# Batch 3's tail tokens by crossbar transpose, in a kernel whose engine orders are written out

## The chip, the cores and the metric

The kernel runs on one core of a Trainium2 chip. The metric is the device time of one execution in microseconds (us). The core has a matrix engine (PE, with its weight loads shown as PEld), a vector engine (DVE), an activation engine (ACT), a general engine (POOL) and a sync engine (SP); SP, ACT and POOL issue DMAs.

## The reference

A sliding-window attention with linear biases feeds an RWKV channel mix. B=8 batches, H=8 heads, S=576 tokens, head size 64; the model width is 512, the inner width 1024.

```python
scores = scale * np.matmul(q, k.transpose(0, 1, 3, 2))
mask = (rel >= 0) & (rel < window)                    # window = 128
scores = np.where(mask, scores + bias[None], -1000000000.0)
attn = np.exp(scores - max); attn = attn / (sum + 1e-09)
x = (attn @ v), heads side by side                    # [B, S, 512]
...
xk = mu_k * x + (1.0 - mu_k) * x_prev                 # x_prev: x one token earlier
xr = mu_r * x + (1.0 - mu_r) * x_prev
k = np.maximum(xk @ w_k, 0.0)
v = k * k @ w_v
r = 1.0 / (1.0 + np.exp(-(xr @ w_r)))
return (r * v)
```

## The kernel before

**Tiles.** 576 tokens are four blocks of 128 and a tail of 64. The attention works by batch and by pair of heads (`g` = 0 to 3). q and k are loaded with the tokens on the partitions, and must be transposed before the scores: batch 0 in two parts and batches 1 to 3 by transposes on PE (`qk_quad`, `qk_some`) and copies by ACT or DVE; batches 4 to 7 by crossbar transposes, which are DMAs on SP's queue (`flip`, L554). `scores` (L742 the products, L748 the biases of batch 0) gives ACT's exponentials (L766); for batches 1 to 7 DVE multiplies with a mask (L779) that ACT makes once (L1198). `attend` multiplies with v and normalizes; the result is transposed (`out_t`, `out_some`, or by crossbar, L928, for batches 5 to 7), shifted and mixed (`shift`), and `channel_mix` does the three matrix products, in 16 calls over pairs of batches. Most matmuls of the program are recorded under L395 and most transposes under L398, which are helpers, and most copies under L715.

**The tail tokens.** The 64 tail tokens of q and k of a batch are loaded by POOL's queue into `ts_buf` (L540; L534 for batch 0). Three ways turn them into `tt_buf`, which `scores` reads for the last block. Batch 0 (`TW`): 32 small matmuls on PE and two copies (`tails`). Batches in `XTT`: one crossbar transpose on SP's queue (`tail_flip`, L647), queued when the batch's loads are planned, ahead of what SP's queue gets for later batches. All others (`tails_full`): four 128x128 transposes on PE and one DVE copy (L715 `tt<-duo`). Both `ts_buf` and `tt_buf` have two buffers.

**What sets the order.** Every step is a node of a planner (`Plan`) with an engine, a planned duration, dependencies and buffers. The nodes of PE, ACT and DVE are numbered in the order in which they are made, and `ORDER` holds three lists of these numbers: each engine does its nodes in exactly that order, and where a node may run on ACT or DVE (squares, some copies), the list that holds it decides. The planner plays the lists through with its durations; from the times that come out follow the buffer numbers and the order of SP's instructions (loads and crossbar transposes in a chain, outputs as they become ready). POOL's loads are in a fixed chain. PE is planned with 0.095 us more where an operation's row grouping (64 or 128 rows of the array) differs from the one before. 82 warm-up matmuls on PE are nodes like others.

The number of hardware DMAs, `n_hw`, counts the crossbar transposes too, `len(XTT)` among them; `n_split = -n_hw % 8` row tiles, counted from the fourth last, are written out in two halves.

Of the kernel before, what the change touches and what calls it, by code (L numbers as in the profile page):

```python
# [20 lines left out]

ORDER = {
    "PE": [int(x) for x in """
# [17 lines left out]
""".split()],  # L41
    "ACT": [int(x) for x in """
# [11 lines left out]
""".split()],  # L54
    "DVE": [int(x) for x in """
# [16 lines left out]
""".split()],  # L72
}

# [168 lines left out]
def kernel(  # L243
# [14 lines left out]
    B, H, S, D = q.shape  # L258
# [15 lines left out]
    PE, ACT, DVE, POOL, SPE, FAB, VIR = "PE", "ACT", "DVE", "POOL", "SP", "FAB", "VIR"  # L274
# [39 lines left out]
    FT = (2, 3)  # L314
    KQ = ACT
    VCUT = True
    XTT = range(4, B)
    VDEP = 0
    TCOST = 1.5
    KLAST = 1  # L320
# [95 lines left out]
    def op(e, dur, deps, prio, emit, need=(), free=()):  # L416
        return plan.add(e, dur, LAT.get(e, 0.2) if isinstance(e, str) else LAT[e[0]] if len(e) == 1 else 0.22,
                        deps, prio, emit, need, free)
# [71 lines left out]
    n_ident = dve_op(0.11, emit_ident, [n_iota], (0, -1))  # L490
# [118 lines left out]
    th, tl, n_w, src1 = {}, {}, {}, {}  # L609
# [341 lines left out]
    def tails(b, prio):  # L951
        htt = Hold("tt")
        hs = th[b]
        if b in XTT:
            plan.follow(last["tt"], ttg[b])
            last["tt"] = ttg[b]
            return tth[b], ttl[b]
        if b not in TW:
            return tails_full(b, prio, htt, hs)
        hp = [Hold("p"), Hold("p")]  # L960

        def bank(r):
            return one(hp[r])[:, 0:256].rearrange("p (g i c n) -> p g i c n", g=G, i=2, n=4)

        def emit(e):
            for i in range(2):
                for n in range(4):
                    for hl, r in ((0, 0), (1, 1), (1, 0), (0, 1)):
                        rows = slice(64 * r, 64 * r + 64)
                        matmul(  # L970
                            hp[r], bank(r)[64 * hl:64 * hl + 64, :, i, :, n],
                            lhsT=ts_buf[hs.idx][rows, 4 * i + n],
                            rhs=ident[rows, rows].rearrange("p (c g t) -> p t g c", g=G, t=2)[:, hl],
                            start=True, stop=True)

        t = op(PE, 0.009 * 32, list(tl[b]) + [n_ident], prio + (0,), emit, hp, [hs])
        t.rows = (65, 65)
        g = virtual("tt", [htt])
        c = [op(DVE, dve_t(256), [t, g], prio + (0,), lambda e, r=r: copy_of(
            hp[r], e, tt_buf[htt.idx][:, :, 0:2, 32 * r:32 * r + 32],  # L980
            one(hp[r])[:, 0:256].rearrange("p (g i w) -> p g i w", g=G, i=2)),
                (), [hp[r]]) for r in range(2)]
        return htt, c
# [146 lines left out]
    for part in range(2):  # L1130
# [3 lines left out]
        for g in range(G):  # L1134
            prio = (0, 0, part, g)
# [12 lines left out]
            hp = Hold("p") if part == 0 else None  # L1148
# [15 lines left out]
            else:  # L1164
                cold = 1.8 if part == 0 and g < 2 else 1.0
                t = op(PE, (0.115 if f32 else 0.0565) * 4 * cold, cs + [n_ident], prio + (3,), emit_t,
                       [hp] + ([hq0[g]] if part == 0 else []))
# [72 lines left out]
    for b in range(1, B):  # L1240
# [4 lines left out]
        for g in range(G):  # L1245
            prio = (0, b, 0, g)
# [77 lines left out]
```

## Time and profile before

| | |
|---|---|
| median of 3 runs | 227.4 us (226.96 to 227.56) |
| the profiled execution's own time | 226.97 us |
| its span, first to last instruction | 225.1 us |
| granted PE clock | 1.00 |
| busy: PE, DVE, ACT, POOL | 217.7, 186.8, 153.0, 91.9 us |
| matmul instructions on PE | 2525 |
| tail crossbar transposes (L647), PE tail transposes of 128x128 (L398 on `ts`) | 4, 12 |

The profile's times are of one execution, counted from the start of its span. A row of the timeline gives start, length, engine, line, operation and tiles of merged instructions; matmuls are pipelined, so the length of a group runs to the modelled end of its last one, and the distance from its start to the next group's start is what it costs PE. Some matmul records are missing, which looks like a short idle time on PE.

### The profile page before, as it was taken

How to read it: one execution, taken by the hardware profiler on the slowest of the kernel's cores; microseconds unless marked ns; L12 is line 12 of the kernel's file. 1: busy time of each engine (PE TensorE's matmuls, PEld its weight loads, DVE VectorE, ACT ScalarE, POOL GpSimd, SP SyncE). 2: the span in 40 equal slices, each digit the busy share in tenths (PEclk: the TensorE clock that was granted, in tenths of full speed). 3: DMA queues.
4: the chain of work that ended last, by engine and by line, in shares of the span. 5: the costliest groups of instructions: out<-in, count | busy, mean ns of one | idle time of the engine just before them, and what ended most of it. 6: DMA issues, size and time to landing. Idle time of an engine off the chain costs nothing.

```text
span 225.1 us, 6344 instructions
## 1 busy us (share of the span) xinstructions
PE 217.7 (97%) x2525; PEld 131.5 (58%) x2555; DVE 186.8 (83%) x422; ACT 153.0 (68%) x276; POOL 91.9 (41%) x118
## 2 busy tenths in 40 slices
PE   8999999999999999999999999999999999999994
PEld 8666756756765555555665565446664655456542
DVE  5779898899768998999789996599969989957433
ACT  2488999898999886980899665843469654135801
POOL 8865726589980983374428663400000000000000
PEclk9999999999999999999999999999999999999999
DMA  7999999999999999999999999999952121243015
GB/s 169 177 186 200 195 197 175 227 146 178 185 154 148 161 149 156 150 182 133 207 207 142 152 181 155 148 180 191 206 167 76 51 57 30 79 155 126 3 41 192
DMA packets 132093, 33.85 MB, mean 150 GB/s; under 512 B 119256, under 2 KB 127712, under 8 KB 132064
## 3 DMA queue, kind: packets, MB, share of 16 engines
q0 software_dynamic: 95728, 16.26, 96.5%
q1 hardware_dynamic: 34592, 16.59, 36.6%
q10 hardware_dynamic: 1744, 0.59, 1.1%
q8 instruction: 20, 0.33, 0.6%
q14 instruction: 9, 0.07, 0.1%
HBM read 33.56 MB, written 9.44 MB: 191 GB/s over the span
## 4 chain that ended last, share of the span: by engine, by line
PE 91%; ACT 4%; DVE 2%; issue 1%; DVEq 0%
PE duo L395 77%; PE duo L742 7%; PE duo L398 4%; PE duo L748 2%; ACT at L766 1%; ACT xt L715 1%; ACT rl L1022 1%; ACT qk L715 1%; DVE ot L1054 1%; DVE qk L715 1%; ACT kk L994 0%; DVE at L779 0%; ACT rs L1040 0%; DVE tv L499 0%; DVE tt L715 0%
## 5 line engine op out<-in xcount | busy, mean ns | idle before, releaser
L1022 ACT ACTIVATE rl<-duo 128x256 bf16<-128x256 f32 (+2 forms) x104 | 47.3, 485 | 34.8 <-PE duo L395 25.1
L395 PE MATMUL duo<-xk,wk_sb 128*128 128x256 bf16 (+2 forms) x410 | 70.2, 312 | 0.3
L766 ACT ACTIVATE at<-duo 128x1024 bf16<-128x1024 f32 (+2 forms) x68 | 63.8, 987 | 8.9 <-PE duo L742 8.5
L395 PE MATMUL duo<-wv_sb,kk 128*128 128x512 bf16 (+2 forms) x281 | 66.1, 373 | 1.1 <-issue 0.5
L395 PEld LDWEIGHTS <-wk_sb 128*128 128x128 bf16 x416 | 38.9, 98 | 22.9 <-issue 0.8
L395 PEld LDWEIGHTS <-kk 128*128 128x128 bf16 x296 | 27.1, 98 | 29.8 <-issue 1.3
L779 DVE TENSOR_TENSOR at<-at,mask 128x1024 bf16<-128x1024 bf16 x56 | 37.2, 680 | 5.8 <-ACT at L766 5.7
L519 POOL DMA_DIRECT2D vs<-in_v_dram x32 | 28.4, 901 | 22.7 <-PE duo L395 16.8
L996 DVE TENSOR_TENSOR kk<-rl 128x256 bf16<-128x256 bf16 (+2 forms) x95 | 29.9, 336 | 8.4 <-ACT rl L1022 8.3
L395 PE MATMUL duo<-wr_sb,xr 128*128 128x512 bf16 x135 | 35.5, 379 | 0.5
L1040 ACT ACTIVATE rs<-duo 128x512 bf16<-128x512 f32 x36 | 21.6, 612 | 19.8 <-PE duo L395 17.1
L1054 DVE SCALAR_TENSOR_TENSOR ot<-rs,duo 128x512 f32<-128x512 bf16 (+2 forms) x37 | 24.3, 665 | 9.1 <-PE duo L395 8.9
L819 DVE TENSOR_TENSOR xu<-duo,rc 128x640 bf16<-128x640 f32 (+2 forms) x36 | 26.2, 738 | 0.4
L913 DVE SCALAR_TENSOR_TENSOR xk<-dl,mu_sb,xt 128x576 bf16<-128x576 bf16 (+1 forms) x32 | 24.6, 779 | 0.2
L913 DVE SCALAR_TENSOR_TENSOR xr<-dl,mu_sb,xt 128x576 bf16<-128x576 bf16 (+1 forms) x32 | 24.6, 778 | 0.0
L395 PEld LDWEIGHTS <-at 128*128 128x128 bf16 x576 | 21.5, 97 | 4.8 <-issue 0.3
L395 PE MATMUL duo<-vs,at 128*128 128x65 bf16 x512 | 21.7, 193 | 0.0
L395 PEld LDWEIGHTS <-xr 128*128 128x128 bf16 x144 | 13.3, 98 | 12.9 <-issue 0.4
L550 POOL DMA_DIRECT2D cb<-in_k_dram x20 | 17.8, 926 | 7.3 <-DMA vs<-in_v_dram 7.2
L550 POOL DMA_DIRECT2D cb<-in_q_dram x20 | 17.7, 931 | 5.6 <-DMA vs<-in_v_dram 2.5
L715 ACT COPY qk<-duo 128x512 bf16<-128x512 bf16 (+1 forms) x25 | 14.5, 593 | 0.4 <-PE duo L398 0.4
L906 DVE TENSOR_TENSOR dl<-xt 128x576 bf16<-128x576 bf16 (+1 forms) x32 | 13.4, 438 | 1.1 <-ACT xt L715 0.6
(73 smaller groups left out, 189.4 us busy)
## 6 DMA issues: line engine op xcount, KB each, us to landing
out_dram<-ot SPq DMA_DIRECT2D x34, 256.0 KB, 4.7
vs<-in_v_dram POOLq DMA_DIRECT2D x32, 128.0 KB, 8.5
cb<-in_q_dram POOLq DMA_DIRECT2D x20, 128.0 KB, 9.8
cb<-in_k_dram POOLq DMA_DIRECT2D x20, 128.0 KB, 11.2
wk_sb<-in_moe_w_k_dram POOLq DMA_DIRECT2D x2, 512.0 KB, 8.7
cb<-in_q_dram POOLq DMA_DIRECT2D x4, 256.0 KB, 9.7
cb<-in_k_dram POOLq DMA_DIRECT2D x4, 256.0 KB, 9.7
wv_sb<-in_moe_w_v_dram POOLq DMA_DIRECT2D x2, 512.0 KB, 12.2
```

What stands on the lines that cost most here:

```text
L395: return use(h, nc.tensor.matmul(*a, **k))
L519: return dma(POOL, 256, issue_t(1024), lambda e: nc.gpsimd.dma_start(out=vs_buf[h.idx][:, j, :, 0:D], in_=v[b, :, 128 * j:128 * j + 128].r ...
L550: return [dma(POOL, 256, issue_t(1024), lambda e, r=r: nc.gpsimd.dma_start(out=cb_buf[h.idx][:, i, r], in_=src[:, :, r]), [g], kind="q") f ...
L715: return (nc.scalar.copy if e == ACT else nc.vector.tensor_copy)(out=out, in_=in_)
L766: lambda e, ah=ah, w=w, hp=hp: nc.scalar.activation(out=ah(), in_=two(hp)[:, :, 0:w], func=AF.Exp, scale=float(scale)), (), [hp])
L779: nc.vector.tensor_tensor(out=a, in0=a, in1=m, op=ALU.mult)
L819: use(hp, nc.vector.tensor_tensor(out=out_, in0=a5()[:, :, :, 0:D], in1=rc[:, :, 0:nt, None].to_broadcast([128, 2, nt, D]), op=ALU.mult), hx)
L913: lambda e: nc.vector.scalar_tensor_tensor(out=buf[hk.idx][:, g, e0 + c0:e0 + c1], in0=dls(), scalar=mu[:, g:g + 1], in1=xc(1), op0=ALU.mu ...
L996: nc.vector.tensor_tensor(out=out, in0=in_, in1=in_, op=ALU.mult)
L1022: a = op(ACT, act_t(n), [s], pr, lambda e, hp=hp, hr=hr: use(hp, nc.scalar.activation(out=rl_buf[hr.idx][:, 0:n], in_=one(hp)[:, 0:n], fun ...
L1040: lambda e, hp=hp, hs=hs: use(hp, nc.scalar.activation(out=rs_buf[hs.idx], in_=one(hp), func=AF.Tanh, scale=0.5), hs), [hs], [hp])
L1054: use(hv, nc.vector.scalar_tensor_tensor(out=ot_buf[ho.idx][:, a:b], in0=rs_buf[hs.idx][:, a:b], scalar=1.0, in1=one(hv)[:, a:b], op0=ALU. ...
```

## The change

`XTT` takes in batch 3, so `tails(3)` returns the crossbar's result and `tails_full` is left for batches 1 and 2. The planned duration of batch 0's tail matmuls rises from 0.288 to 0.5 us; their instructions stay. With batch 3's two tail nodes gone, all numbers from 579 on fall by two, and all three lists are new: PE's has 450 numbers in place of 451, ACT's 282 in place of 281, DVE's 420 in place of 422. Nine nodes that may run on either engine go from DVE to ACT and eight the other way. The order of the late PE nodes within a batch, and of batches among each other, differs nearly everywhere by a few places; the last four nodes of PE are the same. `n_split` becomes 0.

```diff
 ORDER = {
     "PE": [int(x) for x in """
-84 109 92 74 83 70 64 40 43 115 97 106 59 80 62 102 110 47 81 100 50 65 105 91 117 103 60 77 93 49 79 112 72 63
-71 82 75 48 42 67 58 85 68 76 52 46 123 86 56 57 39 69 53 55 116 108 90 163 125 78 89 120 126 139 161 119 113
...
-221 243 279 223 192 273 264 276 209 340 226 261 258 270 328 361 343 373 295 326 313 287 331 282 376 334 364 284
...
+101 57 106 51 86 85 92 49 79 82 113 100 74 65 50 102 80 108 64 68 41 76 66 39 40 91 72 98 99 55 70 105 93 114 52
+75 58 54 59 94 107 63 118 77 61 87 47 46 104 78 123 62 67 81 97 120 112 89 110 125 126 88 115 96 56 137 161 149
...
+226 276 243 279 209 189 270 340 328 264 261 192 267 326 361 373 343 273 307 287 292 282 364 346 331 289 284 367
...
     "ACT": [int(x) for x in """
...
     "DVE": [int(x) for x in """
...
@@ -314,7 +314,7 @@
     FT = (2, 3)
     KQ = ACT
     VCUT = True
-    XTT = range(4, B)
+    XTT = range(3, B)
     VDEP = 0
     TCOST = 1.5
     KLAST = 1
@@ -973,7 +973,7 @@
                             rhs=ident[rows, rows].rearrange("p (c g t) -> p t g c", g=G, t=2)[:, hl],
                             start=True, stop=True)
 
-        t = op(PE, 0.009 * 32, list(tl[b]) + [n_ident], prio + (0,), emit, hp, [hs])
+        t = op(PE, 0.5, list(tl[b]) + [n_ident], prio + (0,), emit, hp, [hs])
         t.rows = (65, 65)
         g = virtual("tt", [htt])
         c = [op(DVE, dve_t(256), [t, g], prio + (0,), lambda e, r=r: copy_of(
```

Node 340 is the first q/k transpose group of batch 1, 343 its first scores, 123 the first transposes of batch 0, 39 to 120 the warm-ups.

82 rows, old and new, of the table ORDER are left out of this document.

## The prediction

> **What bounds the kernel now.** I read the page's busy shares and slices first, then the chain, then a table of stages, then the timeline at the places that the change touches.
>
> ```profile
> span 225.1 us, 6344 instructions
> PE 217.7 (97%) x2525; PEld 131.5 (58%) x2555; DVE 186.8 (83%) x422; ACT 153.0 (68%) x276; POOL 91.9 (41%) x118
> PE   8999999999999999999999999999999999999994
> PE 91%; ACT 4%; DVE 2%; issue 1%; DVEq 0%
> ```
>
> The matrix engine (PE) is busy in every slice and carries 91% of the chain. Work that leaves PE is worth its own time; work that leaves another engine is worth something only where PE waits for that engine. The stage table says where that can be (columns after the length: busy us and instructions of PE, weight load, DVE, ACT, POOL):
>
> ```profile
> core 0: us, PE busy (x) PEld busy (x) DVE busy (x) ACT busy (x) POOL busy (x), PEclk, DMA share, GB/s
> 0.00:13.00 13.00, 11.74 (x168) 9.68 (x168) 8.55 (x41) 5.03 (x7) 10.60 (x20) 1.00 1.30 178
> 13.00:20.00 7.00, 6.68 (x147) 4.10 (x136) 5.97 (x22) 6.13 (x16) 4.28 (x6) 1.00 1.64 189
> 20.00:25.00 5.00, 5.00 (x107) 4.39 (x109) 4.55 (x15) 4.89 (x14) 3.24 (x4) 1.00 1.56 191
> 25.00:30.00 5.00, 4.52 (x157) 3.58 (x148) 4.76 (x15) 5.00 (x14) 3.19 (x4) 1.00 1.30 205
> 30.00:45.00 15.00, 14.73 (x193) 9.38 (x194) 13.61 (x29) 13.86 (x27) 7.78 (x10) 1.00 1.71 199
> 45.00:60.00 15.00, 14.67 (x275) 8.88 (x277) 13.45 (x25) 14.26 (x29) 14.05 (x17) 1.00 2.25 166
> 60.00:90.00 30.00, 29.63 (x390) 18.00 (x394) 26.21 (x54) 25.70 (x45) 19.44 (x24) 1.00 1.89 156
> 90.00:150.00 60.00, 59.48 (x597) 33.34 (x605) 53.12 (x108) 44.69 (x70) 29.33 (x35) 1.00 1.81 167
> 150.00:221.00 71.00, 70.42 (x530) 39.65 (x538) 55.80 (x117) 33.05 (x63) 0.00 (x0) 1.00 0.48 104
> ```
>
> From 13 to 60 us PE, ACT and DVE are all about full: ACT has 5.00 of 5 us at 25 to 30 and 14.26 of 15 at 45 to 60. PE's idle time, length less busy, is 0.32 + 0.00 + 0.48 at 13 to 30, 0.27 + 0.33 at 30 to 60, and 0.37 + 0.52 + 0.58 after 60; in the first 13 us it is 1.26, most of it ahead of the first matmul. So all that new lists can win behind 13 us is about 2.9 us, and less, because a good part of the 1.47 us after 60 is records of matmuls that are missing. That ceiling matters more than anything else here: a reordered program does the same PE work.
>
> **The change part by part.** *The tail tokens of batch 3.* Four 128x128 transposes on PE and one DVE copy go, one crossbar transpose on SP's queue comes. PE and then DVE at that place:
>
> ```profile
> 59.82 0.82 PE L395 MATMUL duo<-xk,wk_sb 128*128 128x256 bf16 x6
> 60.48 0.39 PE L398 MATMUL duo<-ident,ts 128*128 128x128 bf16 x4
> 60.70 0.60 PE L395 MATMUL duo<-xk,wk_sb 128*128 128x256 bf16 x4
> 60.90 0.42 DVE L715 COPY tt<-duo 128x512 bf16<-128x512 bf16 x1
> ```
>
> The four hold PE from 60.48 to 60.70: 0.22 us, all on the path, since PE stands back to back there. The copy takes 0.42 us of DVE, in a stage in which DVE has 26.21 of 30 us: its cover is those 3.8 us of slack, and I cost its removal at nothing (at most 0.42 if DVE were the bound there). The loads of the tail tokens stay with POOL's queue.
>
> *The crossbar transpose that comes.* The landing times, a load, and the place of the consumer:
>
> ```profile
> tt<-ts SPq DMA_TRANSPOSE x4, 6.8
> qx<-cb SPq DMA_TRANSPOSE x32, 7.7
> 53.56 0.76 POOL L540 DMA_DIRECT2D ts<-in_k_dram  x1
> ts<-in_k_dram POOLq DMA_DIRECT2D x8, 64.0 KB, 8.7
> 74.93 0.47 PE L398 MATMUL duo<-ident,xu 64*128 64x64 bf16 x20
> ```
>
> Batch 3's second tail load is issued at 53.6 and by the median has landed at 62.3; 6.8 us more is 69.1. In the new PE list the first batch 3 scores that read the tail (node 596 in the new numbers) stand two places ahead of the transposes of batch 2's outputs (node 493), which the old run made at 74.93. That leaves some 5 us, so the transfer is hidden. What it stands in front of is batch 4's own crossbar queue, which is the first rival.
>
> *One output less.* `n_split` is worked out from the number of hardware DMAs; 95 becomes 96, so it goes from 1 to 0 and the fourth row tile from the end leaves in one DMA and not two. Nothing waits for either: 0.
>
> *Changes of PE's row grouping.* Going through both PE lists with the node's row counts, operations on 64 rows follow ones on 128, or the other way round, 89 times before and 92 times after. The price of one:
>
> ```profile
> 215.81 4.05 PE L395 MATMUL duo<-wv_sb,kk 128*128 128x512 bf16 x18
> 93.22 1.02 PE L395 MATMUL duo<-xk,wk_sb 128*128 128x512 bf16 x4
> 94.17 0.56 PE L742 MATMUL duo<-qx 64*128 64x256 bf16 x8
> ```
>
> Eighteen equal matmuls in 4.05 us with a last one of about 0.37 give 0.216 us from start to start. Four would be 0.865; the 64-row operation starts 0.95 after the first, so a change costs 0.09 us. Three more are +0.28. This eats what the four transposes give.
>
> [...]
>
> *The tail transposes of batch 0.* Only the planner's duration changes (0.288 to 0.5); the instructions are the same. What the shorter value cost:
>
> ```profile
> 16.01 0.65 PE L395 MATMUL duo<-ident,ts 64*64 64x32 bf16 x32
> 16.72 0.34 PE L742 MATMUL duo<-qk 64*128 64x128 bf16 x4
> 17.25 0.60 PE L748 MATMUL duo<-dist,sid 128*128 128x256 bf16 x4 [0.20 <-DVE tt L715]
> ```
>
> They hold PE for 0.47 us (16.01 to the next operation at 16.48), and the copies behind them arrive late: 0.20 us idle by the row; from start to start 16.72 to 17.25 is 0.53 us for about 0.2 of matmuls, so 0.3 lost. The wait is for the banks that these transposes hold until DVE has copied them. A planner that knows 0.5 puts what needs new banks later; the new PE list has an output transpose right behind, and the next bias group after that. So I expect this wait to shrink or go.
>
> *The new lists, up to the first scores of batch 1.* This is where a bound other than PE decides. In the old run those scores start here:
>
> ```profile
> 0.99 4.53 PE L395 MATMUL duo<-warm 128*128 128x128 bf16 x46 [0.99 <-DVE warm L488]
> 26.59 0.66 ACT L715 COPY qk<-duo 128x512 bf16<-128x512 bf16 x1
> 27.87 0.49 ACT qk L715
> 28.39 0.39 PE L742 MATMUL duo<-qk 64*128 64x256 bf16 x4 [0.25 <-ACT qk L715]
> L1198 ACT ACTIVATE mask<-dist 128x256 bf16<-128x256 bf16 x8 | 3.4, 475 | 0.0
> ```
>
> PE waits for ACT, which evacuates the batch's q/k transposes. Between the end of the first-half exponentials and the copy that releases these scores the old ACT list has 34 operations, the new one 36: all eight mask operations (0.475 each) in place of six, two more q/k copies, one Relu and one Square less. That is about 1 us more ACT work ahead of the copy; but the old run's scores start 1.1 us after their own copy has ended (26.59 + 0.66 to 28.39), because ACT still had to empty other banks, and the new list empties those first. So I expect the scores at about 28.3 again, with PE a little further: the new list has one more q/k group and batch 1's tail transposes ahead of them, and one group of four `wk` matmuls less, some 0.1 to 0.2 us more work. At the very start four more warm-ups stand ahead of the first transposes (50, not 46; 0.056 each warm); they fill idle time later in the old list, so I cost them at 0. The stage gives -0.15 by ACT's work and -0.3 by the tail's wait; they are the same microseconds, not a sum. I take -0.3, between 0 and -0.8 (all of the 13 to 30 us idle), or +0.95 if the masks come out of PE's time.
>
> *The new lists, 28 to 60 us.* Idle is 0.60 us in the table. The largest place:
>
> ```profile
> 51.49 0.34 PE L742 MATMUL duo<-qk 64*128 64x256 bf16 x4
> 52.03 0.45 PE L398 MATMUL duo<-ident,cb 64*64 64x64 bf16 x32
> ```
>
> From the first scores at 51.49 PE has 0.2 us of row work until the transposes at 52.03: they wait for free banks while ACT is full. Counted from the lists, behind 13 us seven Squares and copies go from ACT to DVE and six the other way, so no engine is relieved: only the order can help. I take -0.35 of a possible 0 to -0.6. Behind 60 us, where DVE and ACT have slack, -0.1.
>
> *Sum:* -0.22 + 0.28 - 0.3 - 0.35 - 0.1 = about -0.7 us. The profiled execution took 226.97 us (span 225.1 and 1.9 around it), 0.4 below the median of three, 227.4; the sum is a difference, so I put it on the median: **226.7 us**. The 0.3% that a measurement of this kernel can tell from no change is 0.68 us, so this is at its edge.
>
> **The rivals.** *The waits only move (227.3).* Three full engines between 13 and 60 us leave no room: a reordering takes a wait from one bank and gives it to another, and the transposes (-0.22) and changes (+0.28) cancel. For: ACT at 5.00 of 5, and a mask that comes earlier pushes a copy later. Against: the wait at 17.25 comes from a wrong duration, not from a full engine. Chance 0.36.
>
> *Batch 4's crossbar queue comes late (slower, about 228.6).*
>
> ```profile
> 57.03 12.05 SPq L1079 DMA_DIRECT2D out_dram<-ot  x2
> 69.25 5.29 SPq L554 DMA_TRANSPOSE qx<-cb  x4
> 77.98 5.53 SPq L554 DMA_TRANSPOSE qx<-cb  x3
> 91.25 0.61 PE L742 MATMUL duo<-qx 64*128 64x256 bf16 x8
> ```
>
> Seven of its eight transposes are in these rows (5.29/4 is 1.3 us of SP each). The last ends its issue at 83.5, so it is issued near 82.2; 7.7 us later is 89.9, and batch 4's first scores start at 91.25: slack 1.3 us. The new list has less PE work ahead of the first of these scores: batch 3's tail transposes, two groups of `wk` matmuls, a `wr` group and one of output transposes are out, two `wr` groups and one of `wk` in, about 0.5 us. If batch 3's transpose is issued just ahead of 69 us, or holds the crossbar for the next ones, the row slips by its 1.3 us and by a wait for a landing, 1 to 2 us; PE takes its list in order, and everything behind those scores stands. It decides once the slip is over about 0.8 us. For: the thin slack, and outputs share SP's queue. Against: SP has nothing but two outputs from 57 to 69 us, so there is a place for the new one well ahead of the row. Price 0 to 2 us past the slack, say +1.2: 228.6. Chance 0.12.
>
> *ACT's masks come too early (slower, about 228.2).* Two more of 0.475 ahead of the copies of batch 1, with nothing saved in banks: +0.95 on a full ACT, less 0.1 of PE work: 228.2. Chance 0.08.
>
> **How the numbers follow.** Forecast, with some of the waits gone: 0.44. The range reaches from the forecast with nearly all of the idle of 13 to 60 us gone (1.4 + 0.3 after 60, 225.7) to the first slow rival's middle: 225.7 to 228.4; below it and above it I leave about 0.1 each. The likeliest case's own range is 225.7 to 227.0. Faster by over 0.3%: 0.44; within: 0.36; slower: 0.20.
>
> **What would show it.** Right: no L398 ts transposes near 60 us, five L647 transposes, the first issued between 59 and 68 us; the wait on `tt` at 17.25 gone; the first scores of batch 1 near 28.3 with more PE work done; idle at 30 to 60 us under 0.4; PE's last matmul about 0.7 earlier than 221.4. Wrong: a PE wait for a DMA near 90 us (first slow rival), the first batch 1 scores near 29 (masks), or PE idle at 13 to 60 us as large as before.

## The result, and the profile after

The changed kernel takes 226.88 us (median of 20 runs, 225.98 to 227.49); the kernel before, on the same chip, 227.41 us (20 runs, 226.94 to 227.82). The ratio is 0.9977, 95% interval [0.9969, 0.9986]: 0.53 us faster. The interval excludes no change, though the gain is below the 0.3% that the prediction took for the edge. The forecast was 226.7 us. The profiled execution took 226.67 us (span 224.8), 0.30 us less than that of before.

The page of the changed kernel has the span, the busy time of the engines, and the shares of the chain of work that ended last:

```profile
span 224.8 us, 6342 instructions
...
PE 216.7 (96%) x2521; PEld 129.6 (58%) x2551; DVE 185.4 (82%) x420; ACT 152.9 (68%) x277; POOL 92.0 (41%) x118
...
PE 85%; ACT 7%; DMA 2%; issue 2%; DVE 2%; SPq 1%; DVEq 0%; ACTq 0%
```

PE is still the bound; the chain now names ACT for 7% (4% before). The stage table of the changed kernel from 13 us on (columns as in the prediction):

```profile
13.00:20.00 7.00, 7.00 (x170) 4.35 (x170) 5.60 (x19) 6.95 (x18) 4.47 (x7) 1.00 1.63 189
20.00:25.00 5.00, 4.84 (x142) 4.22 (x139) 4.77 (x16) 5.00 (x16) 2.69 (x4) 1.00 1.56 195
25.00:30.00 5.00, 4.42 (x96) 2.90 (x95) 5.00 (x14) 4.99 (x13) 2.99 (x4) 1.00 1.32 201
30.00:45.00 15.00, 14.83 (x222) 9.26 (x223) 12.21 (x29) 13.40 (x26) 8.12 (x11) 1.00 1.70 199
45.00:60.00 15.00, 14.69 (x256) 8.87 (x251) 13.84 (x27) 14.05 (x27) 13.99 (x18) 1.00 2.25 159
```

PE has no idle time left at 13 to 20 us (0.32 before), and more than before at 20 to 30 us (0.16 + 0.58; before 0.00 + 0.48), where ACT has 9.99 of 10 us. At 30 to 60 us the idle time went from 0.60 to 0.48. The timeline of the changed kernel, PE and SP, at the places that the prediction named; behind it the last group of PE in the kernel before:

```profile
15.87 0.65 PE L395 MATMUL duo<-ident,ts 64*64 64x32 bf16 x32
16.45 0.28 PE L398 MATMUL duo<-ident,xu 128*128 128x128 bf16 x2
...
24.47 0.45 PE L398 MATMUL duo<-ident,cb 64*64 64x64 bf16 x32 [0.16 <-ACT xt L715]
27.35 0.40 PE L398 MATMUL duo<-ident,ts 128*128 128x128 bf16 x4 [0.48 <-ACT rl L1022]
28.49 0.39 PE L742 MATMUL duo<-qk 64*128 64x256 bf16 x4
...
60.12 1.98 SPq L647 DMA_TRANSPOSE tt<-ts  x1
...
90.59 0.61 PE L742 MATMUL duo<-qx 64*128 64x256 bf16 x8
...
220.24 1.26 PE L395 MATMUL duo<-wv_sb,kk 128*128 128x384 bf16 x12
```

```profile
220.56 1.26 PE L395 MATMUL duo<-wv_sb,kk 128*128 128x384 bf16 x12
```

Batch 0's tail transposes (first row) are followed without a gap. Two waits that the profile puts down to ACT stand before the first scores of batch 1, which come at 28.49. The new crossbar transpose is issued at 60.12, and batch 4's first scores start at 90.59 with no wait. The last group starts 0.32 us earlier.

### The profile page after: what moved, and what is told of

It reads as the page before. It is cut to its first block, busy times and chain, and to the rows that moved or that the text cites. A ratio compares the mean times of both kernels' runs of the same rounds, so it can differ in the third digit from the quotient of the medians.

```text
span 224.8 us, 6342 instructions
## 1 busy us (share of the span) xinstructions
PE 216.7 (96%) x2521; PEld 129.6 (58%) x2551; DVE 185.4 (82%) x420; ACT 152.9 (68%) x277; POOL 92.0 (41%) x118
## 3 DMA queue, kind: packets, MB, share of 16 engines
q1 hardware_dynamic: 34992, 16.72, 37.5%
## 4 chain that ended last, share of the span: by engine, by line
PE 85%; ACT 7%; DMA 2%; issue 2%; DVE 2%; SPq 1%; DVEq 0%; ACTq 0%
PE duo L395 74%; PE duo L742 7%; PE duo L398 3%; DMA qx<-in_q_dram 2%; ACT at L766 2%; ACT qk L715 1%; ACT xt L715 1%; ACT rl L1022 1%; ACT mask L1198 1%; PE duo L748 1%; SPq L569 1%; DVE ot L1054 1%; ACT rs L1040 0%; DVE tt L715 0%; DVE ot L906 0%
## 5 line engine op out<-in xcount | busy, mean ns | idle before, releaser
L1022 ACT ACTIVATE rl<-duo 128x256 bf16<-128x256 f32 (+2 forms) x104 | 46.2, 483 | 39.5 <-PE duo L395 28.5
L395 PEld LDWEIGHTS <-kk 128*128 128x128 bf16 x296 | 26.6, 98 | 29.0 <-issue 1.9
L996 DVE TENSOR_TENSOR kk<-rl 128x256 bf16<-128x256 bf16 (+2 forms) x97 | 31.0, 337 | 13.2 <-ACT rl L1022 12.7
L395 PE MATMUL duo<-wr_sb,xr 128*128 128x512 bf16 x137 | 36.0, 379 | 0.4
L715 ACT COPY qk<-duo 128x512 bf16<-128x512 bf16 (+1 forms) x28 | 15.0, 588 | 1.4 <-PE duo L398 1.3
```

Of the source, the lines that this page charges most:

```text
L395: return use(h, nc.tensor.matmul(*a, **k))
L715: return (nc.scalar.copy if e == ACT else nc.vector.tensor_copy)(out=out, in_=in_)
L996: nc.vector.tensor_tensor(out=out, in0=in_, in1=in_, op=ALU.mult)
L1022: a = op(ACT, act_t(n), [s], pr, lambda e, hp=hp, hr=hr: use(hp, nc.scalar.activation(out=rl_buf[hr.idx][:, 0:n], in_=one(hp)[:, 0:n], fun ...
```

## The experiments

One pair of profiles says little here, as the last section shows. So I used a number that is worked out from each trace, the **lag**: the start of a PE step in the trace, less the planner's durations of all PE steps ahead of it in the list (batch 0's tail transposes at 0.5 us in every kernel), less 0.095 us, the planner's price, for each change of row grouping so far. Lag grows only where PE takes longer than planned, above all where it waits. The table has the mean lag of the steps that start at 10 to 12 us, and then what it gained up to the steps that start at 20 to 22, 36 to 40, 55 to 60, 62 to 70, 120 to 130 and 210 to 222 us.

| kernel | at 11 | 21 | 38 | 57 | 66 | 125 | 216 |
|---|---|---|---|---|---|---|---|
| before | 0.60 | +0.65 | +1.06 | +0.27 | +0.12 | +0.12 | +0.26 |
| e11, duration alone | 1.06 | +0.61 | +1.07 | +0.23 | +0.15 | +0.10 | +0.26 |
| e1, crossbar alone | 1.42 | +0.62 | +1.05 | +0.23 | +0.36 | +0.36 | +0.25 |
| e10, crossbar and duration | 1.29 | +0.67 | +1.06 | +0.23 | +0.36 | +0.10 | +0.25 |
| e2, lists and duration | 0.90 | -0.20 | +1.46 | +0.26 | +0.04 | -0.05 | +0.85 |
| changed | 0.81 | -0.20 | +1.56 | +0.23 | +0.07 | -0.07 | +0.27 |
| e8, changed, six `ot` | 1.25 | -0.25 | +1.47 | +0.26 | +0.06 | -0.05 | +0.06 |
| e9, changed, output late | 1.41 | -0.26 | +1.49 | +0.26 | +0.06 | -0.05 | +0.11 |

From 11 us on the increments of kernels with the same lists agree to 0.1 us almost everywhere; what differs is the lag at 11 us. There is one profile of each kernel, so differences of 0.1 us in the table mean little.

**The three parts of the change.** First the crossbar tail with the old lists, less the two steps that fall away.

```diff
--- before
-    XTT = range(4, B)
+    XTT = range(3, B)
 # lists: the PE and the DVE step of batch 3's tail taken out, all else in the old order
```

> The old lists with only batch 3's tail nodes taken out and its tail by crossbar transpose. Theory (the transposes' own PE time, 0.22 us, is all that this part gives): 0.1 to 0.3 us faster than before, ratio 0.9987 to 0.9996, no L398 ts transposes near 60 us, later PE work of 61 us on about 0.2 earlier. Rival (the crossbar part is the gain): 0.4 us or more faster, ratio under 0.998. Second rival (crossbar transpose in SP's queue delays batch 4's row): slower, a PE wait near 91 us.

Measured: 227.81 us (before 227.39), ratio 1.0019 [1.0008, 1.003]. The work that leaves PE makes the kernel 0.4 us slower, not 0.2 faster.

Then the opposite: lists and duration of the changed kernel, with the tail of batch 3 on PE again.

```diff
--- changed
-    XTT = range(3, B)
+    XTT = range(4, B)
 # lists: the PE and the DVE step of batch 3's tail put back in at about 60 us
```

> The new lists, with batch 3's tail transposes and copy put back on PE and DVE at about 60 us. Theory (lists give the rest, about 0.3): 0.2 to 0.4 us faster than before, 227.1, ratio 0.998 to 0.999. Rival (the crossbar is the gain): same as before. Second rival (the lists are all of it): 0.5 faster.

Measured: 227.28 us, ratio 0.9999 [0.9986, 1.0011]: the same as before. The first rival had this time, but its reason, that the crossbar is the gain, is ruled out by e1.

Crossbar tail and planned duration, with the old lists:

```diff
--- before
-    XTT = range(4, B)
+    XTT = range(3, B)
...
-        t = op(PE, 0.009 * 32, list(tl[b]) + [n_ident], ...
+        t = op(PE, 0.5, list(tl[b]) + [n_ident], ...
 # lists as in e1
```

> The kernel before with batch 3's tail through the crossbar and the tail transposes of batch 0 planned at 0.5 us, but with its old lists. Theory (the crossbar tail pays only with lists that were laid for it): like the crossbar alone, 227.6 to 228.0 us, since SP's order is the same up to 120 us. Rival (the planned duration, which orders SP's queue, is what the crossbar lacked): 226.9 to 227.3 us.

Measured: 227.49 us (before 227.51), ratio 1.0000 [0.9991, 1.0009], between the two ranges that I had given.

The duration alone. With fixed lists it moves a few outputs on SP's queue, and it gives nine PE steps of the head other banks (the parts of the `duo` tiles that PE writes its results to):

```diff
--- before
-        t = op(PE, 0.009 * 32, list(tl[b]) + [n_ident], ...
+        t = op(PE, 0.5, list(tl[b]) + [n_ident], ...
```

> The kernel before with only the planned duration of the tail transposes changed, 0.288 to 0.5 us; its lists stay, and what moves is the order of a few outputs among the crossbar transposes of batches 4 and 5 on SP. Theory (the head of the program is set by the lists): the wait at 17.25 us stays, 227.2 to 227.6 us; a shift of up to 0.3 us either way would be due to the outputs on SP. Rival (the duration carries the change's gain): 226.8 to 227.1 us.

Measured: 227.35 us, ratio 0.9997 [0.9988, 1.0006]. The time is as expected, but the wait at 17.25 us, which I thought would stay, is gone; the point on the head below says why that gives nothing.

So none of the parts that were run does it alone: duration -0.0003, crossbar and duration 0.0000, lists and duration -0.0001 (each to about 0.001), all three -0.0023. Lists and crossbar without the new duration were not run, so whether the duration is needed beside them stays open. Why the crossbar gives nothing with the old lists is seen by setting e11 (tail on PE) beside e10 (crossbar) at that place: PE, and ACT's two exponentials of the scores ahead. First e11, then e10:

```profile
58.89 0.69 PE L742 MATMUL duo<-qk 64*128 64x256 bf16 x8
59.49 2.02 ACT L766 ACTIVATE at<-duo 128x1024 bf16<-128x1024 f32 x2
60.91 0.39 PE L398 MATMUL duo<-ident,ts 128*128 128x128 bf16 x4
61.58 0.62 PE L395 MATMUL duo<-vs,at 128*128 128x65 bf16 x15
```

```profile
59.18 0.69 PE L742 MATMUL duo<-qk 64*128 64x256 bf16 x8
59.78 2.02 ACT L766 ACTIVATE at<-duo 128x1024 bf16<-128x1024 f32 x2
60.32 1.49 PE L395 MATMUL duo<-xk,wk_sb 128*128 128x256 bf16 x12
61.85 0.62 PE L395 MATMUL duo<-vs,at 128*128 128x65 bf16 x15
```

From the scores to the `vs,at` matmuls are 2.69 us with the four transposes and 2.67 without. In e10 nothing stands between the `wk` matmuls and `vs,at`, yet PE starts `vs,at` 0.23 us later than the pace of the `wk` matmuls would have it (twelve at 0.108 from 60.32 is 61.62). What `vs,at` needs is the end of the second exponential, at 61.80: by the planner's bank numbers it writes the pair of banks that this exponential reads. (It does not need the values, which DVE still has to multiply with the mask.) The transposes had filled a wait for ACT; without them the wait is bare. The table has it twice: +0.36 at 57 to 66 us in e1 and e10, +0.12 and +0.15 with the tail on PE. The profile before had shown it, in ACT's row beside PE's:

```profile
59.05 2.02 ACT L766 ACTIVATE at<-duo 128x1024 bf16<-128x1024 f32 x2
61.14 0.62 PE L395 MATMUL duo<-vs,at 128*128 128x65 bf16 x15
```

The exponentials end at 61.07, so `vs,at` at 61.14 could move by 0.07 us at most, not by 0.22.

Why e1 measured slower than e10 by 0.3 us stays open. e1's profile has 0.26 more lag at 66 to 125 us, nearly all of it in one place: from the `wr` group at 90.21, over batch 4's first scores, to the attend step at 93.69 PE takes 3.48 us in e1, but 3.24 in e10 (90.14 to 93.38) and before (89.43 to 92.67). Those scores read batch 4's crossbar transposes, so this is where e1's second rival and the prediction's first slow one put their wait, here at a fifth of the 1.2 us. No row says what PE waits for, and there is one profile of each.

With the new lists PE has other work at this place (`wk` and `wr` groups between the two attend steps), the lag grows by 0.04 to 0.07 only, and there the crossbar tail is worth 0.4 to 0.5 us (e2 to changed, by the times and by the ratios). That is more than its 0.22 us; e2's profile has a wait that the changed kernel's lacks. ACT and PE in e2, then PE in the changed kernel:

```profile
130.57 0.60 ACT L1040 ACTIVATE rs<-duo 128x512 bf16<-128x512 f32 x1 [2.58 <-DVE ot L1054]
131.22 0.62 PE L395 MATMUL duo<-vs,at 128*128 128x65 bf16 x15 [0.64 <-ACT rs L1040]
```

```profile
130.42 0.61 PE L395 MATMUL duo<-vs,at 128*128 128x65 bf16 x15
```

ACT waits for DVE's output step, which starts at 129.76 in e2 and at 128.97 in the changed kernel. In e2 that is 0.10 us after an earlier output, issued on SP at 122.81, has landed (129.66); in the changed kernel that output is issued at 122.60 and lands at 128.87, again 0.10 us ahead. (The profile puts DVE's 0.72 us of idle time in e2 down to a PE matmul; that it is the landing is read from the times.) Both stand on SP's queue next to crossbar transposes. This gave a theory: outputs near crossbar transposes hold their `ot` buffer too long.

**More output buffers.** One buffer more, in e2 and in the changed kernel:

```diff
-    NO = 5
+    NO = 6
```

> The new lists with batch 3's tail on PE (lists alone), with six output buffers and not five. In the run with five PE stood 0.64 us at 131.2 behind ACT behind a DVE output that started when an output DMA issued at 122.81 landed at 129.66. Theory (lists alone lost their gain in that one wait): the wait goes, 0.4 to 0.7 us faster than lists alone, 226.6 to 226.9, level with the changed kernel. Rival (the crossbar part is needed for the gain): stays at 227.2 to 227.4.

Measured, in e2: 227.50 us, ratio 1.0001 [0.9985, 1.0018]. The wait at 131 us shrinks to 0.20, and another comes (DVE, PE):

```profile
89.33 0.69 DVE L1054 SCALAR_TENSOR_TENSOR ot<-rs,duo 128x512 f32<-128x512 bf16 x1 [0.75 <-DMA out_dram<-ot]
91.95 0.47 PE L398 MATMUL duo<-ident,xu 64*128 64x64 bf16 x20 [0.34 <-DVE xu L819]
```

Here the profile names the DMA itself: DVE's output step waits 0.75 us for an output that SP issued at 82.10, behind five crossbar transposes, and PE waits behind DVE. So an output's buffer can hold up DVE and PE, but a buffer more does not make the kernel faster: the planner gives out all buffers anew, by its own durations, and the wait comes at another place.

> The changed kernel with six output buffers. Its own output at 128.89 also starts just when an output DMA has landed (128.87), but PE did not stand there. Theory: level with the changed kernel or up to 0.2 faster, 226.7 to 226.9. Rival (the buffer number feeds back through the planner's SP order): another size either way, over 0.3.

Measured, in the changed kernel: 226.81 us, ratio 0.9973 [0.9965, 0.9982], level with the changed kernel.

**One output behind the transposes.** To test the theory I moved one output of the changed kernel from ahead of the last two transposes of batch 4 to behind them.

```diff
--- changed
-                    y = plan.add(SPE, 0.6, 0.0, [d], ...
+                    late_out = 4.0 if row == 5 * 128 else 0.0
+                    y = plan.add(SPE, 0.6, 0.0, [(d, d.lat + late_out)], ...
```

> The changed kernel with one output moved on SP's queue: the fourth of the tiles of rows 512 to 895 that is sent (issued at 79.05 us in the changed kernel, ahead of the last two crossbar transposes of batch 4 and of its tail) is sent behind them, at about 84 us; nothing else moves. Theory (outputs that stand behind crossbar transposes hold their ot buffer too long): it lands at 88 to 91 us instead of 82 to 85, DVE's output step near 89 us waits 0.3 us or more for a DMA out_dram<-ot, PE stands 0.2 to 0.5 us near 92 us, and the time is 227.1 to 227.4 us. Rival (the gain of the whole change is PE's own work and the start, and the place of an output does not count): no such wait on PE, 226.7 to 227.0 us.

Measured: 226.65 us, ratio 0.9966 [0.9953, 0.9978]. SP and DVE:

```profile
83.94 1.34 SPq L647 DMA_TRANSPOSE tt<-ts  x1
85.38 4.26 SPq L1079 DMA_DIRECT2D out_dram<-ot  x3
88.59 0.68 DVE L1054 SCALAR_TENSOR_TENSOR ot<-rs,duo 128x512 f32<-128x512 bf16 x1
```

The output does go behind the transposes, with a landing of 6.7 us (median of the three), and DVE's next output step does not wait. So the place of an output on SP's queue has no price by itself here, and the theory is not borne out as an account of the gain. The run does not test a planner that hands the buffer on too early: told of the delay, as here, it gives the step at 88.59 another buffer. The interval overlaps that of the changed kernel, so neither e8 nor e9 is shown to beat it.

**The head: which order wins at 10 to 22 us.** The new order for all steps that the old plan starts in the first 22.5 us, the old one behind, and the opposite.

```diff
--- before
-        t = op(PE, 0.009 * 32, list(tl[b]) + [n_ident], ...
+        t = op(PE, 0.5, list(tl[b]) + [n_ident], ...
 # lists: those steps in the order of the changed kernel
```

> New lists for the nodes that the old plan starts in its first 22.5 us (batch 0 and the first mixes), old lists behind them, batch 3's tail on PE. Theory (the 0.65 us that the new head gains are lost again where ACT lets batch 1's scores go): PE is 0.5 to 0.7 us ahead of the old run at 20 to 24 us and level with it by 30; total within 0.2 us of before. Rival (the head's gain lasts): 0.5 to 0.7 us faster, 226.8.

Measured: 228.97 us, ratio 1.0064 [1.0047, 1.0081].

```diff
--- changed
 # lists: those steps in the order of the kernel before
```

> The changed kernel with the old order for those same nodes of the first 22.5 us. Theory (the head's gain is lost at batch 1 anyway; transposes and late lists are the gain): 0.3 to 0.5 us faster than before, ratio 0.998 to 0.9987, wait on the batch 0 tail back at 17 us. Rival (the head's gain lasts): same as before or slower.

Measured: 230.65 us, ratio 1.0145 [1.0119, 1.0172]. Neither is within what I expected: both are slower, mostly at the seam, where two orders that were not laid for each other meet. PE in e3, then in e4:

```profile
29.92 0.39 PE L742 MATMUL duo<-qk 64*128 64x256 bf16 x4 [1.38 <-ACT qk L715]
```

```profile
31.64 0.39 PE L742 MATMUL duo<-qk 64*128 64x256 bf16 x4 [1.38 <-ACT qk L715]
```

The total says nothing about the head (and in e4 a part of it is a lower clock, see the last section), but the lag up to the seam does: from 11 to 21 us it is -0.13 in e3 (new order) and +0.63 in e4 (old order), like the table's -0.20 to -0.26 and +0.61 to +0.67. The order of these first steps carries that difference, whatever follows.

**The masks later.** The changed kernel, with three of ACT's mask steps moved from 22 to 24 us to behind the copies and Relus that free PE's banks:

```diff
--- changed
 # ACT list: mask steps 253, 249, 255 taken out ahead of 244 and 210, put in behind 342
 # DVE list: the copy of the masks (256) moved to just ahead of 257
```

> The changed kernel with ACT's three mask steps that stand at 24 to 28 us moved behind the steps that first free PE there, and the DVE copy of the masks moved with them. Theory (the 0.65 us that the new head gains is given back because ACT is full at 24 to 28 us): the PE waits of 0.45 us at 24.5 and 0.48 us at 27.35 us shrink, PE is 0.2 to 0.4 us ahead of the changed kernel from 30 us on, 226.5 to 226.7 us. Rival (the masks are due at once: the copies and the first multiplications with a mask come late in their turn): new waits at 28 to 33 us, 226.9 to 227.4 us.

Measured: 229.37 us, ratio 1.0091 [1.0059, 1.0124]. PE:

```profile
27.54 0.40 PE L398 MATMUL duo<-ident,ts 128*128 128x128 bf16 x4 [0.71 <-DMA ts<-in_k_dram]
30.11 0.39 PE L742 MATMUL duo<-qk 64*128 64x256 bf16 x4 [1.17 <-DVE qk L715]
```

The wait at 24.5 us is gone, but the masks (1.07 us of ACT, now from 26.78) push the copies behind them, and batch 1's first scores come at 30.11, not 28.49: lag +2.48 from 21 to 38 us instead of +1.56. The rival was right, and the cost larger than it said (in part by a lower clock, see the last section). ACT is full at this place, and this other order is worse. The first of the two rows names a second thing that PE needs there, the load of batch 1's tail tokens: it lands at 27.49 here, and at 27.31 in the changed kernel, just when ACT's Relu ends, so that the 0.48 us at 27.35 could be put down to either. The load is not what limits this stage: in e2 and e9 it lands at 26.60 and 26.35, and the lag still grows by 1.46 and 1.49 from 21 to 38 us.

**Other numbers of crossbar tails.** All tails of batches 3 to 7 on PE:

```diff
--- changed
-    XTT = range(3, B)
+    XTT = range(8, B)
 # lists: PE and DVE steps for the tails of batches 3 to 7 put in ahead of their first use
```

> The changed kernel with the tails of batches 3 to 7 all on PE (four transposes and one DVE copy each, about 4 us ahead of their use), no tail crossbar transposes: the part of the change five times over and backwards. Theory A (a tail on PE costs its own 0.22 us wherever PE is full): 1.1 us more than the changed kernel, 228.0. Theory B (what a crossbar transpose does to SP's queue and to the landing of outputs matters more than PE's 0.22): any other size, most likely under 0.5 more, or faster than the changed kernel.

Measured: 229.60 us, ratio 1.0093 [1.008, 1.0106]: 2.7 us above the changed kernel, where theory A said 1.1. Five tails are 1.13 us of planned work and two grouping changes more 0.19 at the planner's price; the rest are mainly waits at 93 to 127 us, where the changed kernel has none, as on PE:

```profile
93.72 0.61 PE L395 MATMUL duo<-vs,at 128*128 128x65 bf16 x15 [0.46 <-ACT rl L1022]
118.45 1.02 PE L395 MATMUL duo<-wv_sb,kk 128*128 128x512 bf16 x4 [0.24 <-ACT at L766]
```

And batch 2's tail through the crossbar too:

```diff
--- changed
-    XTT = range(3, B)
+    XTT = range(2, B)
 # lists: the PE and the DVE step of batch 2's tail taken out
```

> The changed kernel with batch 2's tail by crossbar as well: the same step once more, four PE transposes at 47.6 us and a DVE copy fewer. Theory A (0.22 us of PE each): 0.1 to 0.3 faster than the changed kernel, 226.7. Theory B (full ACT at 45 to 60 us takes it back, or SP's queue moves): level with it or slower, 226.9 to 227.3.

Measured: 230.58 us, ratio 1.0145 [1.0127, 1.0162]: 3.7 us above the changed kernel, far outside both theories. PE (the scores are L741 in this kernel's text), then a table of PE by stage (us, busy, instructions, granted clock, DMA share, GB/s):

```profile
52.13 0.21 PE L741 MATMUL duo<-tt,qk 64*128 64x64 bf16 x2 [2.01 <-DMA tt<-ts]
```

```profile
50.00:53.00 3.00, 0.99 (x72) 1.00 2.10 142
53.00:55.00 2.00, 1.84 (x16) 0.63 2.41 157
55.00:57.00 2.00, 2.00 (x8) 0.52 2.40 157
```

SP issues that transpose at 46.16, and it lands 6 us later; PE waits 2.01 us for it. Then the granted clock falls to 0.63 and 0.52, and the 384-wide `wk` matmuls follow each other every 320 ns instead of 162. Batch 3 has the time for the crossbar, batch 2 has not. `XTT` also sets how many row tiles go out in halves (`n_split` is 5 in e5, 7 in e6, 0 in the changed kernel); that does not show in the time, since from PE's last step to the end of the span all three take 3.6 to 3.7 us.

## Why the prediction was right, point by point

The time came within 0.2 us, in the range, and on the expected side; the sum was -0.7 and the medians say -0.53. That it came so near is partly luck, since two terms were mis-sized in opposite directions and one was right for a wrong reason. Step by step:

**Tail transposes, -0.22.** Right as work, wrong as a reason. "All on the path, since PE stands back to back there" failed: with the old lists the same 0.22 us turned into a wait for ACT's exponentials (e10 beside e11). In the new lists, which put other work there, it does become time.

**Grouping changes, +0.28.** Three more, as counted. No run isolates them. The price holds at batch 4's first scores in the changed kernel too: they start 0.95 us after the first of the four 512-wide matmuls ahead (89.64 to 90.59), where the next operation on 128 rows starts 0.86 us after four such matmuls begin (92.85 to 93.71), so 0.09 us; the planner's 0.095 is near it.

**The head, -0.3.** The size is about right, by another way. The wait on `tt` did go, and by the mechanism I gave: with the old order of the head it stands in before (17.25) and e1 (18.05), which plan 0.288, and is absent in e10, e11 and e4, which plan 0.5, because the planner then gives the bias group behind it (L748) a pair of banks that the tail transposes do not hold. But this wins nothing. From the scores at 16.72 to those at 18.75 the kernel before takes 2.03 us, and e10 (17.44 to 19.47) and e11 (17.15 to 19.18) take 2.03 as well: three of the bias groups in between are about 0.1 us later instead. The gain comes from the new order, and the old order has a second place of 0.3 us that I had not seen. It is the same in every profile of that order, as in e10's PE:

```profile
13.84 0.28 PE L398 MATMUL duo<-ident,xu 128*128 128x128 bf16 x2
14.24 0.50 PE L748 MATMUL duo<-dist,sid 128*128 128x384 bf16 x2
```

These are two transposes of 0.056 each, and then 0.29 us of standing. From 11 to 21 us the new order wins 0.8 to 0.9. The table then takes 0.4 to 0.5 back at 21 to 38 us, where ACT is full: I foresaw the scores of batch 1 standing still (28.3; before 28.39, after 28.49), but not that this caps the gain. Net, 11 to 38 us: old order +1.67 to +1.73, new order +1.22 to +1.36, so -0.43.

**28 to 60 us, -0.35.** This step failed. From 38 to 57 us the lag grows by 0.23 to 0.27 in all kernels of the table: no gain. Idle time at 30 to 60 us is 0.48, not under 0.4. Half of a visible idle time is no estimate where three engines are full; I had no row that said which wait the new order would end.

**Behind 60 us, -0.1.** Too small. From 57 to 216 us the lag of before and e11 grows by 0.50 and 0.51, that of the changed kernel by 0.27 and of its variants e8 and e9 by 0.07 and 0.12: -0.23 to -0.44. Which waits the new order ends there, no run isolates. So two mis-sized terms, this one and the one at 28 to 60 us, made up for each other. By the changed kernel's own row the sum is -0.22 + 0.28 - 0.34 + 0 - 0.23 = -0.51 (-0.34 is its +1.36 at 11 to 38 us against the old order's mean of +1.70); the measured difference is 0.53.

**The rivals.** "The waits only move" is what each part of the change does alone: e10, e11 and e2 are at no change. "Batch 4's queue late" did not happen in the changed kernel: the scores at 90.59 have no wait, and the new transpose found its place at 60.12, between two outputs, as the argument against had it. Only e1 may show a trace of it (0.24 us). "Masks too early" had its place right: ACT's waits at 24.5 and 27.35 are there, 0.64 us in all. But in e12 the masks further back cost 2.5 us (1.2 and 1.5 in the two executions at full clock), so they are not too early.

## What to carry to other kernels

An engine that is busy without a gap can still have a wait under its work. Before work that leaves it is counted as time, find the instruction behind it and what that needs from other engines; here four transposes filled a wait of the same length. A wait can also be for the place that a result goes to, not for data, as that of `vs,at` in e10 (0.23 us). An order and the work it was laid for are one change: the parts tried were worth nothing, together they were worth 0.5 us, and a splice of two orders lost 1.6 to 3.8 us. When the effect is smaller than the scatter of the start, compare the growth of the lag by stage over several profiles, not two spans.

## What the hardware showed that I had not expected

**The pace of the first matmuls.** The warm-up matmuls at the start follow each other every 107 ns at first and every 56 ns later. The step between the two lay at 3.63 us in the changed kernel's profile, at 4.80 in that of before, and anywhere up to 6.93 (e9) in the others; the first matmul starts at 0.99 in all eight kernels of the table. PE at 3 to 5 us, in the changed kernel and then in e9, whose heads are the same:

```profile
3.00:5.00 2.00, 2.00 (x33) 1.00 1.05 267
```

```profile
3.00:5.00 2.00, 2.00 (x21) 1.00 1.13 280
```

There are 33 matmuls and 21 in the same 2 us, while the column of the granted clock reads 1.00 for both. What ends the slower pace no run shows; from 3.63 to 6.93 its end is spread over 3.3 us. With the landing of the first loads (e10 waits 0.61 us for one at 8.38) that makes the lag at 11 us 0.60 to 1.42, a spread larger than the whole effect of the change; the profile of before was the luckiest at that place, so the pair of profiles shows 0.30 us where the medians show 0.53.

**One late transfer cost twice in e6.** There PE stood 2.01 us, and the clock was then 0.63 and 0.52 in two stages of 2 us. What the clock gave in these 4 us is 2.3 us at full speed, so the slow stretch costs about 1.7 us, and the two together are the 3.7 us. That the wait brings the lower clock is my reading of their order in time, and no run isolates it: behind the waits of 1.38 us in the profiles of e3 and e4 the mean clock of the whole execution is still 0.999 and 1.000. All four executions of e6 have a mean clock of 0.990 or 0.991. Three of the five of e4 (230.65 to 231.32 us) and four of the six of e12 (229.09 to 230.81) have 0.990 to 0.993 too; the others, at 0.999 or 1.000, took 229.56 and 229.76 (e4), and 228.07 and 228.38 (e12). The profiles of e4 and e12 are of executions at full clock, so they don't show where it falls.
